# The first projection's constants turned by TensorE, and a new order of the opening steps, in a fused attention and feed-forward kernel

## The chip, the cores and the metric

One core of one Trainium2 chip runs the whole kernel. The metric is the device time of one execution in microseconds; three executions before the change took 102.31, 102.52 and 102.64 us, median 102.52. Beside these stands one profiled execution of 102.53 us, whose span (from the first to the last recorded instruction) is 100.8 us; all durations below are from it. Engines are named as the profile does: PE (TensorE), DVE (VectorE), ACT (ScalarE), POOL (GpSimd) and SP (SyncE, whose queue issues most transfers).

## What is computed

```python
def _attn_ref(q, k, v, S1, S2):          # q, k, v: (4, 4, 1088, 32); S1, S2: (8, 32)
    def phi(x):
        a = np.einsum('rd,bhsd->bhsr', S1, x)
        b = np.einsum('rd,bhsd->bhsr', S2, x)
        return np.einsum('bhsi,bhsj->bhsij', a, b).reshape(*x.shape[:-1], r * r)
    q_p, k_p = (phi(q), phi(k))
    kv = np.einsum('bhsf,bhsd->bhfd', k_p, v)
    z = np.sum(k_p, axis=2)
    num = np.einsum('bhsf,bhfd->bhsd', q_p, kv)
    den = np.einsum('bhsf,bhf->bhs', q_p, z)[..., None] + 1e-06
    return num / den

def _moe_ref(x, w_in, w_out, beta):      # x: (4352, 128); w_in: (128, 2048); w_out: (2048, 128)
    h = x @ w_in
    g = h * (1.0 / (1.0 + np.exp(-beta * h)))
    return g @ w_out
```

The attention's output, with its four heads side by side, is the x of the feed-forward part. Inputs and output are float32.

## The kernel before

The attention runs batch by batch (four batches), and the feed-forward part over 9 chunks of 512 tokens, the last of 256, as soon as their tokens are in xT. The order of all work is written out by hand as a string of names (SEQ, line 1005); each name calls a function that issues its instructions, and each engine takes its own in that order. "+" is `first` (one wave: two matmuls of xT with w_in, line 435, and the activation g on ACT, line 444; nothing if no tokens are ready), "-" is `second` (two matmuls of g with w_out, line 411), "~" is one idle matmul of 448 columns (line 196), whose result nobody reads. Ten such matmuls also stand at the very start.

Batch 0 has an opening of its own. S1 and S2 come in 128 rows each (the 8 rows repeated 16 times; `load_s`, line 102, one on ACT's queue and one on POOL's, followed on ACT's by beta in 48 rows). DVE turns each in blocks of 32 (`prep_s`, line 266); POOL multiplies it with a mask into sk, the weights of the key projection; ACT spreads it into s0 and s1, the weights of the query projections. DVE turns k (`turn_k`, line 470, in two parts), PE projects it with sk (`kps`, line 507), DVE turns the result into kab (`kab`, line 543, two instructions), and POOL and DVE form the outer products kp (`outer`, line 555). From kab PE also sums gram (line 646), from which z follows (zt, zc, zb, lines 650 to 670). On the query side DVE turns q (`turn_q`, line 476), PE makes aps and bps (`spread`, line 593), DVE and ACT copy aps and DVE multiplies (`mult`, line 613); den (line 675) with `invert` (line 688) and `spread_rc` (line 705) gives the reciprocals, `num0` (line 711) the numerators, and `divide0` (line 724) writes xT. Queries of batch 0 go in two chunks, A and B.

Beta is split into three bf16 parts (`beta_top` on ACT, line 286, and `beta_left` on POOL and then DVE, line 289), spread over 128 rows by PE in four groups of four matmuls (`beta_part`, line 294) and copied by ACT (`beta_copy`, line 305, 512 columns each). POOL multiplies it into w_in (`prep_win`, line 314), a quarter each; w_out is scaled by 1/beta on ACT or DVE (`prep_wout`, line 335; on ACT two instructions per name).

PSUM is handed out by three helpers: `two` (a pair of banks, one at a time), `one` (one bank), and `wave2` (two pairs in turn, which the waves use as well). A tile from a helper waits until what was there before has been read. On SP's queue a transfer can also wait for an earlier transfer, since eight semaphores are used in turn.

Steps of the opening by name: tk00 and tk01 turn k's two parts, tqa and tqb q's; kp0, ka0 are the key projection and its turn; bt, bl, be, bc are beta's split, spread and copy; o00 to o04 the outer products, v00 to v04 kv of batch 0; aa, ba, ca, ma the query products of chunk A, da and ia its den and reciprocals, ab, bb, cb, mb those of chunk B; lv, lk, lq, lw, lo and lb load v, k, q, w_in, w_out and beta for the scaling.

Of the kernel before, what the change touches and what calls it, by code (L numbers as in the profile page):

```python
# [18 lines left out]
def kernel(  # L19
# [36 lines left out]
    JR = [(0, 2), (2, 4), (4, 6), (6, 9)]  # L56
    JR0 = [(0, 2), (2, 4), (4, 6), (6, 8), (8, 9)]
# [91 lines left out]
    def load_v(b):  # L149
# [3 lines left out]
        for g in range(4):  # L153
# [8 lines left out]
            )  # L162

# [96 lines left out]
    sab = []  # L260
# [3 lines left out]
    st = []  # L264

    def prep_s(n):
        st_ = sb([P, 4, R], F32, f"st{n}")
        nc.vector.transpose(out=st_.rearrange("p u r -> p (u r)"), in_=sr[n])
# [3 lines left out]
        sab.append(t.rearrange("p i j -> p (i j)"))  # L272
        st.append(st_)

    def prep_sq():
        for t in sq:
            for n in range(2):
                nc.gpsimd.tensor_copy(out=t[:, R * n : R * n + R], in_=st[n][:, 0, :])
# [15 lines left out]
    def beta_part(i):  # L294
        t = PS["beta", i] = two("betaps")[:, 0]
        for n in range(NU):
            nc.tensor.matmul(  # L297
                out=t[:, CB * n : CB * n + CB],
                lhsT=cut(bsel, [[0, P]], NU * i + n),
# [5 lines left out]
    def beta_copy(i):  # L305
        nc.scalar.copy(out=beta_bc[:, WP * i : WP * i + WP], in_=PS["beta", i])  # L306
# [188 lines left out]
    def project(t, moving):  # L495
        for g in range(4):
            for pi in range(2):
                rows = slice(64 * pi, 64 * pi + 64)
                nc.tensor.matmul(  # L499
                    out=t[32 * g : 32 * g + 32, pi, :JW],  # L500
# [6 lines left out]
    def kps(b, new=two):  # L507
        t = PS["kps", b] = new("kps")
        kT = kT2[b % 2]
        project(t, lambda rows, g: kT[rows, NJK * g : NJK * g + NJK, :])  # L510
# [15 lines left out]
    def left_copy(j0, j1, eng):  # L526
        if 0 not in KPS:
            KPS[0] = two("left")[:, 0]
        eng(
            out=KPS[0][:, R * H * j0 : R * H * j1],  # L530
            in_=KAB[0][:, 0, j0:j1].rearrange("p j h i -> p (j h i)"),
        )

    def turn_ab(t, name):
        o = sbA.tile([P, 2, NJK, H, R], F32, tag=name, name=name)
        for pi in range(2):
            nc.vector.transpose(  # L537
                out=cut(o, [[R * H, NJK], [NJK * H * R, 2], [1, 2 * R]], 2 * R * pi),
                in_=t[:, pi, :JW].rearrange("p (j n c) -> p j n c", j=NJK, n=2),
            )  # L540
        return o

    def kab(b):
        KAB[b] = turn_ab(PS["kps", b], "kab")
# [10 lines left out]
    def outer(dst, b, src, nm, j0, j1, eng=None):  # L555
        if b not in dst:
            dst[b] = sbA.tile([P, NJK, H, F], F32, tag=nm, name=nm, bufs=1)
        a0 = src[b][:, 0, j0:j1]
        n = H * (j1 - j0)
        left = cut(a0, [[R, n], [1, R], [0, R]])  # L560
        if b == 0 and eng is nc.vector:
            left = cut(KPS[0], [[R, n], [1, R], [0, R]], R * H * j0)
        (eng or nc.vector).tensor_tensor(  # L563
            out=cut(dst[b][:, j0:j1], [[F, n], [R, R], [1, R]]),
            in0=left,
            in1=cut(a0, [[R, n], [0, R], [1, R]], NJK * H * R),
# [67 lines left out]
    def sums(t, ab, n):  # L634
        for j in range(NJK):
            c = 32 * (j % 4)
            nc.tensor.matmul(  # L637
                out=t[c : c + 32, : H * R],
                lhsT=ab[:, n, j].rearrange("p h i -> p (h i)"),
                rhs=ab[:, 1 - n, j].rearrange("p h i -> p (h i)"),  # L640
# [5 lines left out]
    def gram(b):  # L646
        PS["gram"] = t = one("gram")
        sums(t, KAB[b], 0)
# [87 lines left out]
    def gram_g(b, own):  # L736
        t = PS["gp", b] = one("gp") if own else PS["kps", b][:, 0, JW:]
        sums(t, KAB[b], 1)
# [7 lines left out]
    def wz_g(b):  # L746
        for h in range(H):
            nc.tensor.matmul(
                out=PS["gp", b][32 * h : 32 * h + 32, 64 : 64 + R],
                lhsT=sr[1],  # L750
# [78 lines left out]
    def d_A():  # L829
        PS["dA"] = one("dps")  # L830
# [81 lines left out]
    do("kp0", kps, 0)  # L912
    do("ka0", kab, 0)
# [136 lines left out]
```

## Time and profile before

| what | number | where it is read |
|---|---|---|
| median of three runs | 102.52 us | runs |
| the profiled execution | 102.53 us | its own time |
| its span | 100.8 us | page, first line |
| PE busy | 94.5 us, 94% | page, part 1 |
| ACT busy | 78.6 us, 78% | page, part 1 |
| DVE busy | 58.7 us, 58% | page, part 1 |
| POOL busy | 35.3 us, 35% | page, part 1 |
| idle matmuls, line 196 | 24, in 8.0 us | groups of instructions |
| waves, line 435 | 144 matmuls, 40.5 us | groups of instructions |
| w_out matmuls, line 411 | 128, 36.1 us | groups of instructions |
| activation g, line 444 | 68, mean 1026 ns | groups of instructions |
| first wave | 16.47 us | timeline |

Times of instructions are counted from the start of the span. The records of PE are pipelined: several float32 matmuls stand beside each other, and a group's length in the timeline, not the sum of its records, tells how long PE was at it. A float32 matmul leaves two records. "Idle before" is the time in which an engine had nothing to do, with the one that ended it.

### The profile page before, as it was taken

The numbers are of one execution on the slowest core, as the hardware profiler recorded it, in microseconds if no ns is written. First come the engines' busy times: TensorE is split into PE (matmuls) and PEld (weight loads), VectorE is DVE, ScalarE is ACT, GpSimd is POOL, SyncE is SP. The second block draws the span as 40 slices with busy tenths as digits, with TensorE's granted clock in tenths as the row PEclk, the third lists the DMA queues.
The fourth block names the chain that finished last, engine by engine and source line by source line (L and its number), as shares of the span: only waits on it lengthen the run. The fifth ranks groups of instructions, "written<-read, shape, count | busy, mean of one in ns | idle before, by whom it ended". The sixth has DMA issues, their size and how long they took to land.

```text
span 100.8 us, 2932 instructions
## 1 busy us (share of the span) xinstructions
PE 94.5 (94%) x1215; PEld 46.1 (46%) x1215; DVE 58.7 (58%) x119; ACT 78.6 (78%) x101; POOL 35.3 (35%) x50
## 2 busy tenths in 40 slices
PE   5999998899999999999999999999999999999930
PEld 2435652334645444354455345454534444446820
DVE  2757997769999986596779399395160020200220
ACT  1523655999999979699997679999679999999920
POOL 5348958676009502939991002800000000000000
PEclk9999999999999999999999999999999999999999
DMA  2899999999601585048200150033003314023141
GB/s 44 301 233 311 350 392 381 203 288 268 125 15 24 86 229 218 7 79 188 65 0 0 20 91 0 0 57 54 0 4 53 53 35 71 0 46 61 26 79 52
DMA packets 22876, 11.35 MB, mean 113 GB/s; under 512 B 18320, under 2 KB 20688, under 8 KB 22864
## 3 DMA queue, kind: packets, MB, share of 16 engines
q1 hardware_dynamic: 22480, 11.06, 43.5%
q8 instruction: 9, 0.15, 0.6%
q10 hardware_dynamic: 352, 0.11, 0.4%
q14 instruction: 3, 0.02, 0.1%
q0 software_dynamic: 32, 0.02, 0.1%
HBM read 8.95 MB, written 2.23 MB: 111 GB/s over the span
## 4 chain that ended last, share of the span: by engine, by line
PE 85%; ACT 6%; DVE 3%; issue 1%; DVEq 0%; ACTq 0%
PE wave L435 29%; PE moeout L411 25%; PE kvz L196 7%; ACT g L444 5%; PE kvz L624 5%; PE nps L791 5%; PE kps L499 3%; PE qps L517 2%; PE betaps L297 1%; PE nps L716 1%; PE aps L600 1%; PE dps L679 1%; PE ndps L673 1%; PE gp L637 1%; PE bps L600 1%
## 5 line engine op out<-in xcount | busy, mean ns | idle before, releaser
L444 ACT ACTIVATE g<-wave 128x1024 f16<-128x1024 f32 x68 | 65.5, 1026 | 5.9 <-PE wave L435 5.4
L435 PE MATMUL wave<-xT,winp 128*128 128x512 f16 (+1 forms) x144 | 40.5, 369 | 0.7 <-DVE xT L728 0.3
L411 PE MATMUL moeout<-g,woutp 128*128 128x512 f16 x128 | 36.1, 379 | 0.0
L435 PEld LDWEIGHTS <-winp 128*128 128x128 f16 x144 | 15.0, 115 | 16.7 <-issue 5.4
L411 PEld LDWEIGHTS <-woutp 128*128 128x128 f16 x128 | 12.2, 98 | 14.2 <-issue 0.9
L421 DVE STREAM_TRANSPOSE o_sb<-moeout 128x512 f32<-128x512 f32 x8 | 5.7, 712 | 19.7 <-PE moeout L411 19.6
L563 POOL TENSOR_TENSOR kp<-kab 128x512 f32<-128x512 f32 (+2 forms) x13 | 14.4, 1138 | 7.5 <-DVE kab L537 5.9
L576 POOL TENSOR_TENSOR qo<-qab 128x512 f32<-128x512 f32 (+1 forms) x9 | 11.5, 1304 | 15.1 <-DVE qab L772 15.0
L587 DVE STREAM_TRANSPOSE qt<-qo 128x512 f32<-128x512 f32 (+1 forms) x12 | 8.9, 760 | 1.5 <-POOL qo L576 1.4
L196 PE MATMUL kvz<-idle 128*128 128x448 f16 x24 | 8.0, 477 | 1.1 <-DVE idle L99 1.1
L624 PE MATMUL kvz<-kp,v 128*32 128x64 f32 x288 | 5.7, 221 | 0.0
L624 PEld LDWEIGHTS kvz<-kp,v 128*32 128x32 f32 x288 | 4.5, 110 | 2.5 <-issue 1.6
L317 POOL TENSOR_TENSOR winp<-w_in_sb,beta_bc 128x512 f16<-128x512 f32 x4 | 5.0, 1275 | 1.5 <-DMA w_in_sb<-in_moe_w_in_dram 1.5
L477 DVE STREAM_TRANSPOSE qT<-q 128x1088 f32<-128x1088 f32 (+2 forms) x5 | 5.3, 1062 | 0.0
L471 DVE STREAM_TRANSPOSE kT<-k 128x1088 f32<-128x1088 f32 (+2 forms) x5 | 5.2, 1036 | 0.0
L549 DVE STREAM_TRANSPOSE qab<-qps 128x576 f32<-128x576 f32 x6 | 4.3, 761 | 1.2 <-PE qps L517 1.1
L196 PEld LDWEIGHTS <-idle 128*128 128x128 f16 x24 | 2.8, 125 | 4.6 <-issue 2.9
L791 PE MATMUL nps<-qt,nd 32*32 32x288 f32 x192 | 4.8, 412 | 0.0
L537 DVE STREAM_TRANSPOSE kab<-kps 128x288 f32<-128x288 f32 x8 | 3.3, 456 | 2.3 <-PE kps L499 2.3
L331 ACT ACTIVATE woutp<-w_out_sb,rbeta 128x128 f16<-128x128 f32 x12 | 4.0, 392 | 0.0
L813 ACT CAST xT<-nps 128x576 f16<-128x576 f32 x4 | 2.6, 640 | 1.8 <-PE nps L791 1.7
L306 ACT COPY beta_bc<-betaps 128x512 f32<-128x512 f32 x4 | 2.4, 588 | 1.4 <-PE betaps L297 1.2
(97 smaller groups left out, 71.0 us busy)
## 6 DMA issues: line engine op xcount, KB each, us to landing
v<-in_v_dram SPq DMA_DIRECT2D x15, 144.0 KB, 7.3
k<-in_k_dram SPq DMA_DIRECT2D x3, 544.0 KB, 5.5
q<-in_q_dram SPq DMA_DIRECT2D x3, 544.0 KB, 9.0
out_dram<-o_sb SPq DMA_DIRECT2D x20, 64.0 KB, 1.9
w_out_sb<-in_moe_w_out_dram SPq DMA_DIRECT2D x2, 512.0 KB, 9.6
w_in_sb<-in_moe_w_in_dram SPq DMA_DIRECT2D x2, 256.0 KB, 6.4
w_in_sb<-in_moe_w_in_dram SPq DMA_DIRECT2D x1, 512.0 KB, 6.2
k<-in_k_dram SPq DMA_DIRECT2D x1, 288.0 KB, 3.0
```

What stands on the lines that cost most here:

```text
L196: nc.tensor.matmul(out=kvz0[:, F:], lhsT=idle, rhs=cut(idle, [[0, 7], [1, F]]), start=fresh, stop=True, skip_group_check=True,)
L411: nc.tensor.matmul(out=moe["acc"][:, :tw], lhsT=woutp[:, j, :], rhs=g[jj], start=(j == 0), stop=(j == NJ - 1),)
L421: nc.vector.transpose(out=o_sb[:, :nt, :].rearrange("p t d -> p (t d)"), in_=moe["acc"][:, :tw])
L435: nc.tensor.matmul(out=wv[:, jj // per, o : o + tw], lhsT=win_unit(j0 + jj), rhs=xT[:, t0 : t0 + tw], start=True, stop=True,)
L444: nc.scalar.activation(out=g[:, :, :gw], in_=wv[:, :, :gw], func=ACTF.Silu)
L471: nc.vector.transpose(out=kT2[b % 2][:, t0:t1].rearrange("p t s -> p (t s)"), in_=k_t[b][:, t0:t1].rearrange("p t d -> p (t d)"),)
L477: nc.vector.transpose(out=qT2[b % 2][:, t0:t1].rearrange("p t s -> p (t s)"), in_=q_t[b][:, t0:t1].rearrange("p t d -> p (t d)"),)
L563: (eng or nc.vector).tensor_tensor(out=cut(dst[b][:, j0:j1], [[F, n], [R, R], [1, R]]), in0=left, in1=cut(a0, [[R, n], [0, R], [1, R]], NJ ...
L576: eng.tensor_tensor(out=cut(QO[b][:, j0:j1], [[F, n], [R, R], [1, R]]), in0=cut(a0, [[32, n], [1, R], [0, R]]), in1=cut(a0, [[32, n], [0, ...
L587: nc.vector.transpose(out=QT[b][:, j0:j1].rearrange("p j h c s -> p (j h c s)"), in_=QO[b][:, j0:j1].rearrange("p j h f -> p (j h f)"),)
L624: nc.tensor.matmul(out=KVZ[b][32 * h : 32 * h + 32, :F], lhsT=v_t[b][:, h, j, :], rhs=KP[b][:, j, h, :], start=(j == 0), stop=(j == NJK - ...
L791: nc.tensor.matmul(out=tiles[g // 2][32 * h : 32 * h + 32, g % 2, :JW], lhsT=ND[b][rows, fc, 32 * h : 32 * h + 32], rhs=QT[b][rows, :, h, ...
```

## The change

S1 and S2 are loaded once, 8 rows each, into one tile of 16 rows. PE turns it with four small matmuls against the unit matrix, one for each group of 32 rows, into one PSUM bank; DVE multiplies that with the mask into sk in one instruction, and ACT spreads s0 and s1 from it. S2 in 128 rows, which a later step needs (`wz_g`), is loaded by itself on SP's queue. The first key projection comes in two parts of 4 and 5 blocks of columns with PSUM banks of their own (`kps0`), and its turn in two as well; kab of later batches is one instruction instead of two. Beta is spread in two groups of eight matmuls into two banks each and copied in two instructions of 1024 columns. den of chunk A goes into the bank pair of `two`. The left copy covers the second part alone. SEQ is written anew from end to end: 20 idle matmuls instead of 24, w_out's first half loaded ahead of q's second part, bl0 to BL1 ahead of kab on DVE, k's turn of batch 1 behind chunk A's division, three scalings of w_out on ACT and one on DVE ahead of the first wave.

```diff
+    KJ = [(0, 4), (4, NJK)]
-    sr = []
+    s16 = sb([2 * R, D], F32, "s16")
+    sr2 = sb([P, D], F32, "sr2")
     def load_s():
-        for n, s_ in enumerate((S1, S2)):
-            t = sb([P, D], F32, f"sr{n}")
-            (nc.scalar, nc.gpsimd)[n].dma_start(
-                out=t,
-                in_=bass.AP(
-                    tensor=s_.tensor, offset=s_.offset, ap=[[0, P // R], [D, R], [1, D]]
-                ),
-            )
-            sr.append(t)
+        nc.scalar.dma_start(out=s16[:R], in_=S1)
+        nc.gpsimd.dma_start(out=s16[R:], in_=S2)
...
+    def load_s2():
+        nc.sync.dma_start(
+            out=sr2,
+            in_=bass.AP(tensor=S2.tensor, offset=S2.offset, ap=[[0, P // R], [D, R], [1, D]]),
+        )
...
+    def turn_s():
+        t = PS["st"] = one("st")
+        for g in range(4):
+            nc.tensor.matmul(
+                out=t[32 * g : 32 * g + 32, : 2 * R],
+                lhsT=s16,
+                rhs=ident[: 2 * R, : 2 * R],
+                start=True,
+                stop=True,
+            )
+
+    def prep_sk():
+        nc.vector.tensor_tensor(
+            out=sk,
+            in0=cut(PS["st"], [[R, 2], [0, 2], [1, R]]),
+            in1=cut(hm, [[0, 2], [R, 2], [1, R]]),
+            op=MUL,
+        )
     def prep_s(n):
-        st_ = sb([P, 4, R], F32, f"st{n}")
-        nc.vector.transpose(out=st_.rearrange("p u r -> p (u r)"), in_=sr[n])
-        nc.gpsimd.tensor_tensor(out=sk[:, n], in0=st_[:, :2, :], in1=hm, op=MUL)
         t = sb([P, R, R], F32, f"s{n}")
-        nc.scalar.copy(out=t, in_=cut(st_, ([[1, R], [0, R]], [[0, R], [1, R]])[n]))
+        nc.scalar.copy(out=t, in_=cut(PS["st"], ([[1, R], [0, R]], [[0, R], [1, R]])[n], R * n))
...
     def beta_part(i):
-        t = PS["beta", i] = two("betaps")[:, 0]
-        for n in range(NU):
+        t = PS["beta", i] = (wave2, two)[i]("betaps")
+        for n in range(2 * NU):
...
     def beta_copy(i):
-        nc.scalar.copy(out=beta_bc[:, WP * i : WP * i + WP], in_=PS["beta", i])
+        w = 2 * WP
+        nc.scalar.copy(
+            out=beta_bc[:, w * i : w * i + w].rearrange("p (m c) -> p m c", m=2),
+            in_=PS["beta", i],
+        )
...
+    def kps0(n):
+        j0, j1 = KJ[n]
+        w = 32 * (j1 - j0)
+        t = PS["kpj", n] = (two, wave2)[n]("kps")
+        project(
+            lambda g, pi: t[32 * g : 32 * g + 32, pi, :w],
+            lambda rows, g: kT2[0][rows, NJK * g + j0 : NJK * g + j1, :],
+        )
...
-    def kab(b):
-        KAB[b] = turn_ab(PS["kps", b], "kab")
+    def kab(b, n=0):
+        t, nj = (PS["kps", b], NJK) if b else (PS["kpj", n], KJ[n][1] - KJ[n][0])
+        o = sbA.tile([P, 2, nj, H, R], F32, tag=("kab", "kab1")[n], name="kab")
+        nc.vector.transpose(
+            out=cut(o, [[2 * R, 2], [R * H, nj], [nj * H * R, 2], [1, 2 * R]]),
+            in_=t[:, :, : 32 * nj].rearrange("p m (j c) -> p m j c", c=32),
+        )
+        KAB[b, n] = o
...
     def d_A():
-        PS["dA"] = one("dps")
+        PS["dA"] = two("dps")[:, 0]
...
     SEQ = """
-        s0 lv00 tk00 ~ ~ bt0 lv01 s1 tk01 bl0 sq lv02 ~ kp0 ~ ka0 lv03 la o00 ~ ~ ~ tqa ~ gr o02 bt1 ~
-        aa lqb zt lk1 ba ca0 zz o01 o04 BL1 lb CA1 be0 bc0 ~ lw0 ~ ma0 ma1 ~ tqb o03 be1 lw2 bc1 v00 da
-        v01 be2 lw1 v02 v03 ia v04 bc2 kd u0 tk1 be3 ra0 nd nc lo0 ra1 lq1 bc3 ~ na xa0 ab u1 xa1 cb0 +
-        ~ CB1 rb bb mb1 mb0 w0 lo1 + u2 w3 kp1 + ka1 u3 lv1 w2 o11 + g1 o13 W1 gm1 nb wz1 + wm1 o12 db -
+        tk00 lv00 lv01 ~ tk01 bt0 st sk lv02 ~ bl0 kp0 s0 lb kq0 s1 lv03 bt1 BL1 lo0 kz0 be0 o00 ~ lqb
+        ka0 o04 tqa O02 ~ ls bc0 ~ o01 gr la zt lw0 o03 aa ba CA1 ca0 zz ma1 v00 ma0 rb lw1 v01 v02 v03
+        v04 da kd w0 lk1 lw2 ~ w2 u0 ~ nd W1 nc ia be1 ~ tqb bc1 na u1 w3 lq1 ab ra1 ra0 xa0 cb0 ~ xa1
+        lo1 ~ + bb + CB1 tk1 mb1 sq u2 - mb0 kp1 ka1 + u3 + lv1 o13 g1 gm1 lq2 wz1 wm1 + o11 db + nb o12
...
     """
```

In the new names kq0 and kz0 are the second part of the projection and the first part of its turn, st and sk the turn of S on PE and the mask product on DVE, ls the separate load of S2.

More of the change, by code (lines that the diff above doesn't have):

```diff
@@ L526, in left_copy, with kab_at @@
     def left_copy(j0, j1, eng):
-        if 0 not in KPS:
-            KPS[0] = two("left")[:, 0]
+        KPS[0] = two("left")[:, 0]
         eng(
             out=KPS[0][:, R * H * j0 : R * H * j1],
-            in_=KAB[0][:, 0, j0:j1].rearrange("p j h i -> p (j h i)"),
+            in_=KAB[0, 1][:, 0].rearrange("p j h i -> p (j h i)"),
         )
[L534 to L541, printed above, removed]
-    def kab(b):
-        KAB[b] = turn_ab(PS["kps", b], "kab")
+    def kab(b, n=0):
[4 more added lines that the diff above has]
+            in_=t[:, :, : 32 * nj].rearrange("p m (j c) -> p m j c", c=32),
+        )
+        KAB[b, n] = o
+    def kab_at(b, j):
+        n = int(b == 0 and j >= KJ[0][1])
+        return KAB[b, n], j - KJ[n][0] if b == 0 else j
     def qab(b):
@@ L911 @@
         do2(f"bl{n}", beta_left, (n,), POOL, DVE)
-    do("kp0", kps, 0)
-    do("ka0", kab, 0)
-    do2("la", left_copy, (0, NJK), ACT.copy, DVE.tensor_copy)
+    for n in range(2):
+        do(("kp0", "kq0")[n], kps0, n)
+        do(("kz0", "ka0")[n], kab, 0, n)
+    do("st", turn_s)
+    do("sk", prep_sk)
+    do("ls", load_s2)
+    do2("la", left_copy, KJ[1], ACT.copy, DVE.tensor_copy)
     for g in range(4):
@@ L992 @@
         for n, (j0, j1) in enumerate(JR):
[L993 removed]
+            do2(f"o{b}{n}", lambda b, j0, j1, e: outer(KP, b, "kp", j0, j1, e), (b, j0, j1), POOL, DVE)
             do2(f"p{b}{n}", lambda b, j0, j1, e: outer_q(b, j0, j1, e), (b, j0, j1), POOL, DVE)
```

70 lines of the change are left out of this document (38 added, 32 removed).

## The prediction, made before the changed kernel had run

> **What bounds the kernel now.** First the page: 100.8 us span, a full granted clock in every slice, TensorE (PE) busy 94%, ScalarE (ACT) 78%. The share is an average, so the second view is the table of stages (busy time of each engine in a stretch, then clock, DMA share, GB/s).
>
> ```profile
> 5.00:10.00 5.00, 5.00 (x87) 2.24 (x85) 3.12 (x8) 1.41 (x5) 3.19 (x8) 1.00 1.08 270
> 10.00:15.00 5.00, 4.81 (x121) 3.11 (x125) 4.77 (x10) 3.07 (x8) 3.99 (x5) 1.00 1.06 373
> ...
> 17.00:28.00 11.00, 10.67 (x210) 4.76 (x209) 8.91 (x18) 10.46 (x20) 5.75 (x5) 1.00 0.93 222
> 28.00:38.00 10.00, 10.00 (x112) 4.82 (x117) 8.92 (x14) 8.92 (x11) 4.07 (x3) 1.00 0.41 97
> 38.00:72.00 34.00, 33.93 (x529) 16.05 (x514) 24.00 (x42) 29.82 (x32) 14.52 (x13) 1.00 0.25 55
> 72.00:90.00 18.00, 17.85 (x84) 8.32 (x82) 3.29 (x6) 16.32 (x18) 0.00 (x0) 1.00 0.20 34
> ```
>
> The first pair of numbers of a row is the stretch's length and PE's busy time. From 28 to 90 us PE lacks 0.22 of 62 us, so the change can't shorten that part; it can only start it earlier or later. Before 17 us PE is busy too, but partly with idle matmuls (line 196) that compute nothing, so there the third view, the timeline, decides (start, length, engine, line, operation; in brackets the idle time before it and who ended it).
>
> ```profile
> 1.06 5.04 PE L196 MATMUL kvz<-idle 128*128 128x448 f16 x13 [1.06 <-DVE idle L99]
> ...
> 5.42 0.21 DVE L268 STREAM_TRANSPOSE st<-sr 128x32 f32<-128x32 f32 x1 [0.61 <-DMA sr<-in_S_dram]
> ...
> 6.03 0.94 PE L499 MATMUL kps<-kT,sk 64*32 64x288 f32 x16
> 6.11 0.40 ACT L287 ACTIVATE bt<-beta_r,bpos 48x128 bf16<-48x128 f32 x1 [1.68 <-DMA beta_r<-in_moe_beta_dram]
> ...
> 7.03 0.85 DVE L537 STREAM_TRANSPOSE kab<-kps 128x288 f32<-128x288 f32 x2 [0.81 <-PE kps L499]
> 7.81 0.67 DVE L477 STREAM_TRANSPOSE qT<-q 128x512 f32<-128x512 f32 x1
> ...
> 8.62 1.12 PE L600 MATMUL aps<-qT,s 32*64 32x256 f32 x32
> 8.75 0.43 DVE L290 TENSOR_TENSOR bq<-br,bt 48x128 bf16<-48x128 f32 x1
> ...
> 10.67 0.59 ACT L306 COPY beta_bc<-betaps 128x512 f32<-128x512 f32 x1
> ...
> 13.50 1.25 DVE L471 STREAM_TRANSPOSE kT<-k 128x1088 f32<-128x1088 f32 x1
> ```
>
> The reader is to see one chain: S lands, VectorE (DVE) turns it, kps, kab, qT, then aps at 8.62. Beta's split (line 287, GpSimd (POOL) in between, line 290) lies beside it: beta_r lands at 6.1, its last step bq stands behind kab and qT on DVE, and nothing before aps needs it. The chain of waits gives 16.47 for the first wave, the point from which PE is fed:
>
> ```profile
> 15.57 0.77 DVE xT L728 x2
> 16.33 0.14 issue
> 16.47 0.60 PE wave L435 x2
> ```
>
> **The change, part by part.** I follow each engine's queue as the changed program has it: an instruction starts when its engine is free and its last input is there, with lengths from these rows.
>
> S. The DVE turns (2 x 0.21) and POOL masks (2 x 0.22) go. PE has 11 idle matmuls ahead of the new turn instead of 13: 11 x 0.388 (5.04/13) from 1.06 ends at 5.33. S lands at 3.9 (issue 0.74 + 3.2) and 5.4 (1.26 + 4.1); eight rows will hardly land later, so PE's queue decides. The turn's four matmuls have no row; between nothing and 0.63 (zc, 16 records), nearest is line 748 (8 records, 0.25): 5.58. The mask product reads PSUM like line 742 (0.19): 5.82. kps, 0.94 in all, split 4:5, ends near 6.9, as before (6.97). So S gains 0.1 at most.
>
> Beta on DVE. bq now stands ahead of both kab parts. Behind beta_r's landing come 0.40 (bt), 0.08 and 0.42 (POOL), 0.07 and 0.40 (bt), 0.03 and 0.43 (bq), with what starts them 1.86. The landing is the unknown: 6.1 as it is (1.43 + 4.7); at the earliest S's 3.2 on the same queue, 4.6. I take 5.8, near its own row, since 120 descriptors fewer go ahead. Then bq ends at 7.66. An early landing helps little: ACT's second bt now stands behind two copies of the turned S (2 x 0.24), which wait for the mask product at 5.82, so bq ends at 7.28 at best, 7.96 at worst. The stall is then kab's: 7.66 + 0.85 = 8.51 instead of 7.88, and qT ends 0.60 later, 9.11.
>
> Beta on PE and ACT. Eight matmuls in a group, 2 x 0.38, from 7.72 to 8.48; one copy of 1024 columns. Bounds: 0.59 (half the columns) and 1.18 (two of them); I take the 1.02 of an ACT instruction of that size (line 444). It ends at 9.57, and aps writes the bank pair that it empties, so aps starts at 9.62 and not behind qT: 1.00 late (0.61 to 1.28 with beta's bounds).
>
> From aps to the first wave, before 16.47 - 8.62 = 7.85. After: aps 1.12; copy 0.69 + 0.08; two products 1.29; den 0.43 + 0.05 (its own bank takes no time off: the five kv groups ahead of it end at 12.65, by zc 0.56 and 1.34, and the products at 12.80); to DVE 0.14; turn and add 0.64, for which the second beta group, in den's bank, waits; that group 0.75 + 0.05; its copy 1.02 + 0.06, for which the second aps waits; aps 0.75 + 0.05; two idle matmuls 0.44. Sum 7.56, first wave at 17.18: 0.29 won back. The won part is k's turn of batch 1 (1.25, row 13.50), which leaves this chain; DVE's q turn (0.77), rb (0.72) and xT (0.76) are done at 16.6, inside it. Net 0.71 late.
>
> Behind the first wave. k's turn now stands ahead of the products that the second kps waits for (17.5 to 18.8): kps at about 19.9, 2.75 behind the first wave instead of 2.36, with one moeout pair (0.43) more done. PE also waits some 0.3 for the first g. I take 0.15 (0 to 0.3). In the tail three wave pairs fewer are left (the built order has 48 ahead of the last projection's second half, not 45), and pairs there take 0.47 where they took 0.43 earlier: -0.1.
>
> Loads. SP now issues w_out's first half (0.5 MB) ahead of q's second part, S2's 128 rows, w_in and k of batch 1, and w_out waits for beta_r as k did. At the 270 to 373 GB/s of the stages q's part comes about 1.5 later, 11.6, needed at 14.3; w_in's first part stays near 12.4, needed by POOL after the outer products (11.9) and by PE at 17.2; k of batch 1 moves from 11.6 to about 15, needed at 17.5. Covered; were they not, each costs its lateness. kab in one instruction (0.75 for 0.85), sq from the copies and the shorter left copy cost nothing: the engines that run them wait at those places.
>
> Sum: 0.71 + 0.15 - 0.1 = +0.76. The profiled execution took 102.53 (span 100.8 and 1.7 around it), the median is 102.52: **103.3 us**, own range 102.7 to 103.9 from the bounds.
>
> **The rivals.** (A) Faster: ACT sets the pace behind the first wave. For it: ACT is busy 10.46 of 11 us from 17 to 28, and six of the twelve scalings of w_out (0.68 for two, 2.0 us) move ahead of the first g, into ACT's waits. If PE's records there only stretch over ACT's work, the stage gets up to 2.0 shorter, and the kernel ends at 102.53 + 0.86 - 2.0 = 101.4; it decides once more than 1.2 of the 2.0 comes through (0.8 of front and 0.4 to be told apart). Against it: the chain of waits stays on PE there but for DVE's 0.75. (B) No change: beta lands by 5.2, the copy takes 0.8 and the second group the same: aps at 9.0, the first wave 0.1 late, 102.6. For it: beta_r's 4.7 is long for 24 KB; against: the S copies hold bt. (C) Slower still: PE's slow start lasts longer. Idle matmuls take 0.388 up to 6.0, then 0.22 (1.12 for five). PE now idles from 6.9 to 7.7; if the step comes after kps and the first beta group, these cost 0.75 x 1.7 more, 104.5; against: the step at 6.0 came after 5 us of matmuls, and 4.3 of them remain. [...]
>
> **How the numbers follow.** Main case 0.60, A 0.16, B 0.14, C 0.10. The range reaches down to A's half, 101.9, and up to 104.2, short of C's full price; about 2 in 10 is outside. Over 0.3% (0.31 us, about what a measurement of this kernel can tell from no change): faster is A, with a little of B, 0.18; same is the rest of B and the main case's low edge, 0.15; slower the rest, 0.67.
>
> **What would show it.** Right: bt's second instruction behind the two S copies; bq directly ahead of kab on DVE, kab near 7.7; PE idle about 0.8 between kps and betaps; aps released by beta's copy at 9.2 to 9.9; first wave at 16.9 to 17.6; PE full from 28 on. Wrong: aps released by qT before 9; a first wave before 16.5; the stretch from the first wave to the second batch's kv shorter than 11 us (then A); idle matmuls of 0.38 behind 6.9 (then C).

## The result, and the profile after

| | median (us) | executions | lowest to highest | ratio to before, 95% interval |
|---|---|---|---|---|
| before, beside it | 102.50 | 4 | 102.31 to 102.64 | |
| after | 104.16 | 4 | 103.85 to 106.39 | 1.0154 [1.0121, 1.0186] |
| before, second measurement | 102.36 | 23 | 102.10 to 102.88, and 104.75 and 134.67 | |
| after, second measurement | 103.91 | 12 | 102.65 to 106.72 | 1.0077 [1.0041, 1.0113] |
| before, beside the second experiments | 102.37 | 23 | 101.94 to 102.80, and 106.28, 107.22, 120.98, 182.35 and 245.68 | |

The change makes the kernel slower, by about 1.5% in the median of all executions and by 0.8 to 1.5% by the two ratios. It also makes it uneven: its executions lie 4% apart, most of those of the kernel before within 0.9%. A ratio counts only executions within 1.5% of their kernel's fastest, so the second one leaves out five of the twelve; below, the median of all executions stands beside each ratio. The forecast was 103.3, in the range 101.9 to 104.2, so the first median lies inside by 0.04 us, and above the 102.7 to 103.9 that the prediction gave to its main case.

The first profiled execution of the changed kernel took 103.85 us with a span of 101.0; the one before had 102.53 and 100.8. So the span is only 0.2 longer, where the sum of the prediction had 0.76 more. The timeline of the changed kernel's front (start, length, engine, line; in brackets the idle time before it and who ended it):

```profile
5.28 0.31 PE L269 MATMUL st<-ident,s 16*32 16x16 f32 x8
...
5.59 0.40 ACT L304 ACTIVATE bt<-beta_r,bpos 48x128 bf16<-48x128 f32 x1 [2.01 <-DMA beta_r<-in_moe_beta_dram]
5.66 0.19 DVE L278 TENSOR_TENSOR sk<-st,hm 128x32 f32<-128x32 f32 x1 [0.56 <-PE st L269]
...
6.53 0.40 ACT L304 ACTIVATE bt<-br,bpos 48x128 bf16<-48x128 f32 x1 [0.32 <-POOL br L307]
...
6.96 0.28 DVE L307 TENSOR_TENSOR bq<-br,bt 48x128 bf16<-48x128 f32 x1 [1.11 <-ACT bt L304]
...
7.17 0.83 DVE L570 STREAM_TRANSPOSE kab<-kps 128x256 f32<-128x256 f32 x2
7.29 0.60 PE L315 MATMUL betaps<-bq,bsel 48*128 48x128 bf16 x8 [0.36 <-DVE bq L307]
...
7.94 1.01 ACT L325 COPY beta_bc<-betaps 128x1024 f32<-128x1024 f32 x1 [1.01 <-PE betaps L315]
...
9.00 0.67 PEld L636 LDWEIGHTS aps<-qT,s 32*64 32x64 f32 x32 [0.23 <-ACT beta_bc L325]
9.00 1.12 PE L636 MATMUL aps<-qT,s 32*64 32x256 f32 x32
...
16.58 0.60 PE L457 MATMUL wave<-xT,winp 128*128 128x512 f16 x2
```

(PEld is TensorE's loading of weights.) The order of the waits is the one that was forecast: bq directly behind beta's second bt, the turn kab and betaps behind bq, aps behind the copy of beta. The times are shorter: TensorE stands 0.36 where 0.8 was expected, aps starts at 9.00 and not at 9.62, the first wave at 16.58, 0.11 behind the 16.47 of before. The chain of waits of the same execution shows that beta's load now heads it (start, length, what):

```profile
1.38 4.12 DMA beta_r<-in_moe_beta_dram
7.68 4.17 POOL kp L599 x4
...
13.80 0.63 PE betaps L315 x8
14.45 1.02 ACT beta_bc L325
15.52 0.75 PE aps L636 x16
```

In the table of stages ScalarE has less to do from 17 to 28 us (9.19 us where it was 10.46), and TensorE's middle is as full as it was (33.95 of 34):

```profile
17.00:28.00 11.00, 10.32 (x142) 3.92 (x142) 9.37 (x17) 9.19 (x14) 5.78 (x5) 1.00 0.83 231
...
38.00:72.00 34.00, 33.95 (x472) 16.14 (x458) 24.34 (x41) 30.32 (x33) 13.36 (x12) 1.00 0.30 59
```

No stage of this execution is 1.3 us longer. What it has more is outside the span: 2.85 us around it instead of 1.73. Of the other executions of the two measurements two have as much around their spans (2.99 and 2.92 us) and the rest 1.78 to 2.13. So most of the median's +1.5 us had to be sought inside the spans of other executions.

### The profile page after: what moved, and what is told of

The parts are those of the page before. It is cut to its first block, busy times and chain, and to the rows that moved or that the text cites. A ratio compares the mean times of both kernels' runs of the same rounds, so it can differ in the third digit from the quotient of the medians.

```text
span 101.0 us, 2967 instructions
## 1 busy us (share of the span) xinstructions
PE 93.6 (93%) x1235; PEld 45.8 (45%) x1235; DVE 59.9 (59%) x117; ACT 78.2 (77%) x99; POOL 33.1 (33%) x46
## 3 DMA queue, kind: packets, MB, share of 16 engines
HBM read 8.93 MB, written 2.23 MB: 110 GB/s over the span
## 4 chain that ended last, share of the span: by engine, by line
PE 74%; ACT 8%; POOL 5%; DMA 4%; DVE 3%; issue 2%; ACTq 1%; DVEq 0%
PE wave L457 30%; PE moeout L433 25%; ACT g L466 5%; PE nps L828 5%; PE kvz L660 4%; POOL kp L599 4%; DMA beta_r<-in_moe_beta_dram 4%; PE qps L551 2%; PE kps L521 2%; PE dps L716 1%; ACT beta_bc L325 1%; PE gp L674 1%; ACT bt L304 1%; PE aps L636 1%; PE ndps L710 1%
## 5 line engine op out<-in xcount | busy, mean ns | idle before, releaser
L466 ACT ACTIVATE g<-wave 128x1024 f16<-128x1024 f32 x68 | 65.7, 1024 | 7.2 <-PE wave L457 6.7
L433 PEld LDWEIGHTS <-woutp 128*128 128x128 f16 x128 | 11.9, 97 | 13.9 <-issue 1.9
L612 POOL TENSOR_TENSOR qo<-qab 128x512 f32<-128x512 f32 (+1 forms) x8 | 10.7, 1360 | 18.7 <-DVE qab L809 18.7
L599 POOL TENSOR_TENSOR kp<-kab 128x512 f32<-128x512 f32 (+2 forms) x12 | 13.5, 1142 | 8.2 <-DVE kab L570 8.1
L443 DVE STREAM_TRANSPOSE o_sb<-moeout 128x512 f32<-128x512 f32 x8 | 5.7, 711 | 16.9 <-PE moeout L433 16.9
L197 PE MATMUL kvz<-idle 128*128 128x448 f16 x20 | 7.0, 489 | 1.1 <-DVE idle L100 1.1
L570 DVE STREAM_TRANSPOSE kab<-kps 128x576 f32<-128x576 f32 (+2 forms) x5 | 3.2, 647 | 1.5 <-PE kps L521 1.5
L197 PEld LDWEIGHTS <-idle 128*128 128x128 f16 x20 | 2.1, 123 | 4.2 <-issue 2.9
L599 DVE TENSOR_TENSOR kp<-kab 128x512 f32<-128x512 f32 (+1 forms) x5 | 3.8, 761 | 0.0
```

The costliest lines, as they stand in the source:

```text
L197: nc.tensor.matmul(out=kvz0[:, F:], lhsT=idle, rhs=cut(idle, [[0, 7], [1, F]]), start=fresh, stop=True, skip_group_check=True,)
L433: nc.tensor.matmul(out=moe["acc"][:, :tw], lhsT=woutp[:, j, :], rhs=g[jj], start=(j == 0), stop=(j == NJ - 1),)
L443: nc.vector.transpose(out=o_sb[:, :nt, :].rearrange("p t d -> p (t d)"), in_=moe["acc"][:, :tw])
L466: nc.scalar.activation(out=g[:, :, :gw], in_=wv[:, :, :gw], func=ACTF.Silu)
L599: eng.tensor_tensor(out=cut(dst[b][:, j0:j1], [[F, n], [R, R], [1, R]]), in0=left, in1=cut(a0, [[R, n], [0, R], [1, R]], nj * H * R), op=MUL,)
L612: eng.tensor_tensor(out=cut(QO[b][:, j0:j1], [[F, n], [R, R], [1, R]]), in0=cut(a0, [[32, n], [1, R], [0, R]]), in1=cut(a0, [[32, n], [0, ...
```

## First experiments: the clock, or the new waits

Two theories came from the prediction: (1) TensorE's clock rises later or unevenly, since it idles near 7 us (the prediction's case C); (2) the waits of the new order cost what they were priced at. Four kernels ran beside each other: the changed one again; it with two idle matmuls more at the start; it with its idle places filled; and the kernel before with four idle matmuls fewer.

```diff
 e2_after_warm12 (from after)
-    WARM0 = 10
+    WARM0 = 12
 e3_after_filled (from after)
-    ... lb kq0 s1 lv03 ...    v01 v02 v03
+    ... lb kq0 ~ ~ s1 lv03 ...    v01 v02 ~ v03
 e4_before_less (from before)
-    s0 lv00 tk00 ~ ~ bt0 ...    o00 ~ ~ ~ tqa
+    s0 lv00 tk00 bt0 ...    o00 ~ tqa
```

> The changed kernel once more, in more executions, to see where the 1.6 us lie: its first profile's span is only 0.25 us longer than before's. Theory 1, PE's clock: PE idles more in the opening and has four idle matmuls fewer, so the step to the full clock (6.0 us before, 6.5 us in the first profile) comes at another place in each execution; then times spread by 1 us or more (first four: 103.85 to 106.39), and the longer the span the later the step or the lower the granted clock. Theory 2, the waits of the new order: the loss stands at the same places in each execution, times within 0.4 us of each other near 104.1, and the profile shows a first wave at 16.6 and a later stall of about 1 us.

> The changed kernel with 12 idle matmuls at the start instead of 10 (as many ahead of the first projection as before the change). They cost 2 x 0.37 us on PE ahead of the turn of S. Theory 1 (clock): the step to the full clock is reached more surely, times lose their spread and the median falls by 0.5 us or more, to 103.6 or less, although the front is pushed 0.7 later. Theory 2 (waits): each step behind S is 0.7 later, the median rises by 0.5 to 0.8, to about 104.8.

> The changed kernel with three idle matmuls in PE's two longest waits of the opening (two behind the second part of the first key projection, one ahead of the fourth kv group), where they cost little: the waits were 0.35 and 0.37 us. Theory 1 (clock): PE counts as busy there, the median falls by 0.5 us or more. Theory 2 (waits): same within 0.3 us, or up to 0.3 slower.

> The kernel before with four idle matmuls fewer (two at the start, two behind kab), 20 as in the changed kernel. Theory 1 (clock): it becomes slower and spread like the changed kernel, 103.3 or more in the median, with single runs over 104. Theory 2 (waits): the first four places were covered by waits for S and qT, so the time stays within 0.3 us of 102.5.

| run | median of all | executions, lowest to highest | ratio | profiled: time, span |
|---|---|---|---|---|
| e1, after again | 103.91 | 12, 102.65 to 106.72 | 1.0077 [1.0041, 1.0113] | 104.90, 103.1 |
| e2, after, 12 idle first | 104.89 | 6, 103.88 to 106.90 | 1.0169 [1.0131, 1.0206] | 103.88, 102.1 |
| e3, after, places filled | 103.89 | 6, 103.55 to 105.49 | 1.0157 [1.0110, 1.0203] | 103.61, 101.8 |
| e4, before, 4 idle fewer | 102.32 | 12, 101.90 to 103.24, and 134.51 | 1.0002 [0.9976, 1.0029] | 101.90, 100.1 |

Neither theory holds. By the trace's clock events the clock rose at 6.52 us in the first profile of after, at 5.08 in e1, 5.29 in e2, 6.50 in e3, and stayed up until TensorE's last matmul was done (in after it fell at 98.68, where the last matmul ends at 97.17; the mean over the span is 0.988, 0.988, 0.994 and 1.0). In the first profile of after idle matmuls start 0.37 us apart ahead of the rise and 0.19 behind it. e1 has the earliest rise of the four and the longest span. Filling the idle places or adding matmuls at the start won nothing, and the kernel before lost nothing by having fewer. But the three new profiles of the changed order have a piece that neither kernel's first profile has. In the chain of waits of e1:

```profile
14.01 0.62 PE betaps L315 x8
14.62 1.22 issue
15.84 0.35 PE kvz L197
...
24.76 0.63 PE nps L753 x12
25.39 0.17 issue
25.56 0.68 PE nps L753 x4
```

of e2:

```profile
13.73 0.51 PE betaps L315 x6
14.24 0.58 issue
14.81 0.28 PE betaps L315 x2
```

and of e3:

```profile
13.86 0.45 PE betaps L315 x5
14.31 0.51 issue
14.82 0.34 PE betaps L315 x3
```

"issue" is time in which the engine waited for nothing that the profile shows. Here it falls ahead of an idle matmul in one run, and between two matmuls of the same group, which depend on nothing new, in the others. Counted from the start of the trace (from nought; an f32 matmul leaves two records, the four of S's turn eight), it is in all three TensorE's matmul record number 220; the second stop of e1 is number 347. That second stop costs more than its 0.17 us, since the ends of matmul records are modelled: the group of 16 takes 1.47 us in e1 and 0.65 in the first profile of after. The 127 matmuls between, with their 127 weight loads, are 254 instructions. The page lists a DMA queue that carries such things:

```profile
q8 instruction: 9, 0.15, 0.7%
```

(of after; packets, MB, share). Each packet is 16,384 bytes, 64.5 for each of the 254. From 28 us on, where the loads are thin, 55 of 75 packets in the fourteen profiles start within a microsecond of the time at which TensorE passes record 93 + 127 n (the others up to 2.2 us earlier or 3.5 later), so a block seems to be asked for when TensorE enters the one before it. The first block would then be asked for at record 93, near 9.3 us, and it starts 2.6 to 4.0 us later in the four profiles of the changed order so far, at a time when the loads keep the 16 DMA engines full (a share of 1.03 to 1.07 from 9.3 to 11.9 us). This gave theory 3: TensorE runs out of instructions where it reaches record 220 before the block is there. By the trace's records of that queue, with runs of the sections below:

| run | block moved (us) | record 220 starts (us) | behind the block's end | stall ahead of it |
|---|---|---|---|---|
| before | 12.72 to 13.82 | 15.40 | 1.58 | none |
| after | 11.90 to 13.00 | 14.34 | 1.34 | none |
| e1 | 13.50 to 14.51 | 15.84 | 1.33 | 1.22 |
| e1, second block (347) | 23.04 to 24.12 | 25.56 | 1.44 | 0.17 |
| e2 | 12.31 to 13.36 | 14.81 | 1.45 | 0.58 |
| e3 | 12.50 to 13.57 | 14.81 | 1.24 | 0.51 |
| e4 | 12.50 to 13.61 | 14.90 | 1.29 | none |
| f1 | 12.03 to 13.11 | 14.54 | 1.43 | none |
| f2 (221) | 13.84 to 14.96 | 16.18 | 1.22 | 0.32 |
| f4 | 12.20 to 13.14 | 15.63 | 2.49 | none |
| g4 (221) | 12.49 to 13.60 | 15.08 | 1.48 | 0.89 |
| g4, second block (348) | 22.91 to 24.25 | 25.54 | 1.29 | 1.72 |
| g5 | 14.23 to 15.34 | 16.69 | 1.35 | 0.37 |

Wherever TensorE stalls, it goes on 1.22 to 1.48 us behind the block's end. Where it doesn't stall, it comes to the record no earlier than that; in f3, g1 and g2, which the table leaves out, it comes 2.4 to 4.4 us behind. Over all block boundaries of the fourteen profiles the shortest distance is the 1.22 of f2. The changed kernel has 20 records more ahead of this place (8 of S's turn, 16 of the projection in two parts, 4 idle matmuls fewer), and so reaches the boundary at 14.3 us instead of 15.4, about when the block is usable; how late that is differs from execution to execution. The stops at a boundary were 0.17 (e1's second) to 1.72 us long (g4's second, in a stretch with a DMA share of 1.03).

## Second experiments: fewer records, more records, S alone

f1 takes the projection back into one part, f3 takes six idle matmuls away as well (four by its expectation), f2 gives the kernel before 21 records more, f4 gives it the part on S alone.

```diff
 f1_after_kps_whole (from after)
-    KJ = [(0, 4), (4, NJK)]
+    KJ = [(0, NJK), (NJK, NJK)]        (kq0, ka0, la leave the order)
 f2_before_24_small (from before)
-    WARM0 = 10
+    WARM0 = 7
+    for _ in range(24):
+        nc.tensor.matmul(out=kvz0[:32, F : F + 8], lhsT=idle[:, :32], rhs=idle[:, :8], ...)
 f3_after_whole_less (from f1)
-    o00 ~ lqb   O02 ~ ls bc0 ~ o01   lw2 ~ w2 u0 ~ nd   be1 ~ tqb
+    o00 lqb     O02 ls bc0 o01       lw2 w2 u0 nd       be1 tqb
 f4_before_s_alone (from before; load_s, load_s2, turn_s, prep_sk, prep_s as in after)
-    s0 lv00 tk00 ~ ~ bt0 lv01 s1 tk01 bl0 sq lv02 ~ kp0 ~ ka0 lv03 la
+    lv00 tk00 ~ ~ bt0 st sk lv01 s0 s1 tk01 bl0 lv02 ~ kp0 ~ ka0 lv03 ls la
```

> The changed kernel with batch 0's first key projection in one part again (8 matmuls of 288 columns, one turn by VectorE, no copy of the left operands); all else as changed. TensorE has 16 matmuls fewer ahead of the first projections of beta and a. Theory 3 (TensorE runs out of instructions: each block of 16,384 bytes is asked for when TensorE enters the block before it, at its matmul number 93, 220, 347 and so on, and comes 5.0 to 6.4 us later, because it waits 2.6 to 4.0 us behind the loads; with the change TensorE needs only 5.0 to 5.3 us for the 127 matmuls between 93 and 220): here the boundary falls 16 matmuls later, on the projection by S of the second half, near 15.5 us, where TensorE waits anyway. Median 102.6 to 103.0, its slowest and fastest execution less than 0.8 apart, no stall without a cause ahead of matmul 220, or one below 0.3. Theory 2 (the waits of the new order cost the time): the order behind the projection is the same, so 103.5 to 104.2.

> The kernel before with three of its ten first idle matmuls replaced by 24 small ones (32 weight columns, 8 columns each), so that TensorE has 21 matmuls more to fetch and about as much work as before; nothing that computes is changed. Theory 3: the instruction block's boundary moves from the projection by S at 15.4 us to an instruction at about 14.1 us, and TensorE stands there for 0.5 to 1.0 us for nothing that the profile shows, ahead of matmul number 220; median 102.9 to 103.6, executions more than 1 us apart. Theory 2 and the theory of the clock: within 0.3 of the kernel before.

> As the run with the key projection in one part, and four idle matmuls behind the projection left out too: 20 matmuls fewer than the changed kernel ahead of the boundary. Theory 3: the boundary lies a little later again, no stall; 102.3 to 102.8, as fast as the kernel before. Theory 2: 103.5 to 104.2. Theory of the clock (idle matmuls keep it at full speed): slower than the run before it, by 0.3 or more.

> The kernel before with the part on S alone: S1 and S2 loaded as 16 rows, turned by four matmuls, one product with the mask on VectorE, the 128-row copy of S2 loaded by SyncE for its later use; projection, beta, den and the order otherwise as before. TensorE has 4 matmuls with one pass more each (8 records) ahead of the boundary. Prediction's own price for this part: a gain of at most 0.1, so 102.3 to 102.5 by that alone. Theory 3: the boundary moves from 15.4 to about 15.0 us, where the block has just landed (13.8 + 1.3 = 15.1): 102.3 to 102.9, with some executions late by a few tenths. Theory 2 sees no wait in this part: 102.3 to 102.5.

| run | median of all | executions, lowest to highest | ratio | profiled: time, span |
|---|---|---|---|---|
| f1 | 103.07 | 12, 102.50 to 105.72 | 1.0051 [1.0025, 1.0077] | 102.50, 100.7 |
| f2 | 103.98 | 8, 103.17 to 105.91 | 1.0158 [1.0127, 1.0188] | 105.04, 102.8 |
| f3 | 104.55 | 12, 102.61 to 107.78 | 1.0077 [1.0035, 1.0119] | 105.03, 103.2 |
| f4 | 103.32 | 6, 102.95 to 103.71 | 1.0099 [1.0069, 1.0128] | 103.28, 101.5 |

f1's median is 0.84 us below the changed kernel's, and its profile has no stall. But the two ratios differ by 0.26% only and their intervals overlap, f1 also takes out a copy and a turn, and three of its twelve executions are still above 104 (theory 3 had allowed a spread of 0.8); so it agrees with theory 3 and doesn't prove it. f2 stalls where it should ("issue" of 0.32 at 15.86, ahead of record 221), but its clock also rose only at 10.16 us (five idle matmuls at 7.65 took 2.05 us, the five of before at 6.90 took 1.12), and nothing here shows why; its loss can be from both, and a cleaner test follows as g4.

f3 was a miss of the kind that teaches. It should have been as fast as before, at 102.3 to 102.8. By the ratios it isn't told apart from f1, but eight of its twelve executions are above 104, where f1 has three. The profiled execution is one of the eight. The stages of its profile (length, busy time of PE, PEld, DVE, ACT and POOL with counts, granted clock, DMA share, GB/s):

```profile
5.77:9.18 3.41, 1.82 (x43) 0.96 (x42) 2.02 (x5) 1.97 (x5) 1.31 (x2) 1.00 1.09 200
9.18:16.01 6.83, 6.33 (x130) 4.16 (x131) 4.45 (x10) 2.39 (x9) 6.49 (x10) 0.50 1.04 391
```

In 3.41 us TensorE was busy for 1.82; then its clock was half for 6.83 us. The mean granted clock goes with the time: 0.925 to 0.983 in the eight late executions, 0.988 to 1.0 in the other four. f1, which has the six idle matmuls that f3 leaves out, has 0.989 to 1.0 in ten of its twelve and 0.983 and 0.958 in the two slowest. So they weren't idle for nothing in this order. The prediction's case C is close to this, but not the same: there the clock rises late, here it falls again. Neither is what the two profiles of the changed kernel show: there the clock stays up until TensorE's last matmul is done. And of the six executions of e1 above 104, five have a granted clock of 0.988 to 1.0, as the others have (0.990 to 1.0); only the latest, 106.72, has 0.980. (In the first measurement one of the four, 104.25, has 0.975.)

f4 has no stall, as its boundary is reached late, and its executions lie close together. It is slower by 1.0% all the same, above the 102.3 to 102.9 expected, by its own order: one idle matmul more than in after stands ahead of the turn, which starts at 5.66 (5.28 in after), and the mask product stands on VectorE ahead of k's second turn, for which the second half of kps waits 0.34:

```profile
5.66 0.30 PE L268 MATMUL st<-ident,s 16*32 16x16 f32 x8
...
6.37 1.21 PE L515 MATMUL kps<-kT,sk 64*32 64x288 f32 x16
...
6.89 0.15 PEld L515 LDWEIGHTS kps<-kT,sk 64*32 64x32 f32 x8 [0.34 <-DVE kT L487]
```

Before, kps started at 6.03 and took 0.94: it ends 0.34 + 0.27 = 0.61 late, and kab (7.65 for 7.03) and the first wave (17.05 for 16.47) follow with it. So S alone, in this order, is no gain, and the run doesn't price it in another.

## Third experiments: beta off the path, and records alone

In the six profiles of the changed order so far beta's first step came between 5.0 and 5.9 us, and in five of them kab 1.58 behind it: a varying load on the path, theory 4. g1 and g2 put bq behind the mask product of the gram sums and both beta groups behind zc, g1 with the projection in one part, g2 in two. g4 is the clean test of theory 3: the kernel before, with its ten first idle matmuls cut in three, as much busy time and 20 records more.

```diff
 g1_whole_beta_behind (from f1), g2_parts_beta_behind (the same from after)
-    PS["beta", i] = (wave2, two)[i]("betaps")
+    PS["beta", i] = two("betaps")
-    bt1 BL1 lo0 kz0 be0 o00 ~ lqb ... tqa O02 ~ ls bc0 ~ o01 gr zt lw0 o03 ... zz ma1 ... ia be1 ~ tqb bc1 na
+    bt1 lo0 kz0 ~ ~ o00 ~ lqb ... tqa ~ O02 ~ ls o01 gr ~ zt lw0 BL1 o03 ... zz be0 bc0 be1 bc1 ma1 ... ia ~ tqb na
 g4_before_idle_in_three (from before)
-    keep_warm(WARM0, True)
+    for n in range(WARM0):
+        for c0, n_, w_ in ((0, 3, 50), (150, 3, 50), (300, 2, 74)):
+            nc.tensor.matmul(out=kvz0[:, F + c0 : F + c0 + n_ * w_], lhsT=idle, rhs=cut(idle, [[0, n_], [1, w_]]), ...)
```

> The changed kernel with the first key projection in one part (as in the run f1_after_kps_whole) and beta moved: its second square on VectorE behind the turn of the projection, the turn of q and the mask product of the gram sums, its 16 matmuls together behind zc (both groups in the same pair of banks), both copies behind them, and three idle matmuls more in the places where TensorE would stand. Theory 4 (beta's load lies on the path of the changed order: it landed between 5.0 and 5.9 us in the profiles taken so far, the turn of the projection follows 1.58 us behind, and where it is late TensorE stands for a microsecond or more near 7 us, in one execution so long that its clock fell to half from 9 to 16 us): with beta off the path the late executions go; first wave at 15.7 to 16.2, median 102.0 to 102.6, fewer than 2 in 10 executions above 103.5. Theory 3 alone (instruction blocks): no better than the run with one part, 102.8 to 103.2, with the same tail to 105 and more.

> The same with the projection in its two parts, as changed: 16 matmuls more ahead of the block boundary (matmul number 220), and otherwise as the run before it. Theory 3: TensorE comes to the boundary near 14 us, before the block is there: a stall of 0.3 to 1.2 for nothing that the profile shows directly ahead of matmul 220, median 102.9 to 103.8, 0.6 to 1.0 above the run before it. Theory 4 alone: as fast as the run before it within 0.3.

> The kernel before with each of its ten first idle matmuls cut into three of 150, 150 and 148 columns: 20 matmuls more to fetch, TensorE busy for as long (3.7 us at half clock), so that its clock has no reason to rise later, and nothing that computes is changed. Theory 3: the block boundary moves from the second projection by S (15.4 us) to near 13.9 us; a stall of 0.3 to 1.2 directly ahead of matmul 220, median 102.8 to 103.6, executions 1 us and more apart. Theory 4 and the theory of the clock: within 0.3 of the kernel before.

| run | median | executions, lowest to highest | ratio | profiled: time, span |
|---|---|---|---|---|
| g1 | 104.91 | 5, 104.90 to 105.24 | 1.0259 [1.0230, 1.0288] | 104.91, 103.1 |
| g2 | 104.76 | 6, 104.32 to 105.61 | 1.0247 [1.0205, 1.0290] | 104.51, 102.7 |
| g4 | 104.80 | 6, 103.67 to 106.90 | 1.0199 [1.0153, 1.0246] | 104.91, 103.0 |

g4 shows theory 3 at work in the kernel before. Nothing that computes is changed and the clock rose at 5.50 us, earlier than before (6.03), yet the kernel is 2.0% slower. Its median of 104.80 is above the 102.8 to 103.6 expected, as the expectation had only the first boundary. Its chain of waits has two in it:

```profile
13.86 0.33 PE ndps L682
14.19 0.89 issue
15.08 0.35 PE kvz L196
...
23.49 0.32 PE moeout L420
23.81 1.72 issue
25.54 0.39 PE moeout L420
```

The stops are ahead of records 221 and 348, 127 apart, 1.48 and 1.29 us behind the ends of their blocks (the table above), and together 2.61 us.

g1 and g2 were meant to test theory 4 and don't, through a wait that they brought in: the second beta group needs the bank pair that the first one's copy empties. In the timeline of g1:

```profile
10.42 0.62 PE L315 MATMUL betaps<-bq,bsel 48*128 48x128 bf16 x8
12.14 0.60 PE L315 MATMUL betaps<-bq,bsel 48*128 48x128 bf16 x8 [1.10 <-ACT beta_bc L325]
```

and in its stages:

```profile
9.77:13.19 3.42, 2.23 (x68) 1.99 (x72) 2.80 (x7) 2.15 (x4) 3.13 (x4) 1.00 1.06 378
13.19:16.60 3.41, 3.41 (x64) 1.69 (x52) 1.16 (x4) 2.27 (x8) 2.68 (x7) 0.50 1.02 407
```

With a stop of 1.10 us TensorE was busy for 2.23 of 3.42 us in that stretch, and the next 3.41 us ran at half clock; g2 is the same (2.31 of 3.41). Such a stretch alone doesn't bring the clock down, though: e1, from 11.91 to 15.32, has 2.33, and g4, around its second stop, has less still, and the clock stayed up in both (1.00 in the second row below; in e1 the two idle matmuls at 17.45 took 0.48, as in after at 16.26, where two took 0.86 in g1's half clock).

```profile
22.57:25.98 3.41, 1.69 (x14) 0.49 (x12) 3.27 (x6) 1.72 (x2) 2.23 (x2) 1.00 1.03 280
25.98:29.39 3.41, 3.41 (x90) 1.72 (x91) 1.66 (x4) 3.00 (x7) 0.00 (x0) 1.00 0.30 67
```

(This view is of g4.) One thing can be read from g2: with beta off the path kab starts at 6.60 and aps at 8.32, where after has 7.17 and 9.00. In these two profiles the change's own beta order costs 0.57 at kab and 0.68 at aps; how much of it reaches the end stays open.

## Last experiment: a version without the two costs

```diff
 g5_whole_less_records (from f1)
-    PS["beta", i] = (wave2, two)[i]("betaps")
+    PS["beta", i] = (two, wave2)[i]("betaps")
-    s16 = sb([2 * R, D], F32, "s16")
+    s16 = sb([2 * R, 4, D], F32, "s16")        (loaded four times over; one matmul turns it)
-    bt1 BL1 lo0 kz0 be0 o00 ~ lqb ... O02 ~ ls bc0 ~ o01 gr zt lw0 o03 aa ba CA1 ca0 zz ma1
+    bt1 lo0 kz0 ~ o00 ~ lqb ... O02 ~ ls ~ o01 gr zt lw0 BL1 o03 aa ba CA1 ca0 zz be0 bc0 ma1
```

> A version meant to keep the change's gains without its two costs: the key projection in one part; S turned by one matmul instead of four (its 16 rows repeated four times in the load); beta's second square on VectorE behind the gram's mask product, its first 8 matmuls behind zc and the other 8 where the changed kernel has them, each group in banks that nothing holds at that time (so that TensorE doesn't stop between them, as it did for 1.1 us in the two runs with beta behind the projection, where its clock then fell to half for 3.4 us); one idle matmul more near the front. TensorE has 21 records fewer than the changed kernel ahead of the same place. Theory 3: the boundary at matmul 220 lies in the second projection by S near 14.7 us, 4.6 to 5.3 us behind its request: a stall of 0 to 0.5, part of it in time in which TensorE waits for the first wave anyway; first wave 15.7 to 16.3; median 101.7 to 102.5, at most 0.2 slower than the kernel before. Theory of the clock: no stop of TensorE above 0.6 us between 6 and 16 us, so no fall; if there is one, 104 and more. Theory 2 (the other waits of the new order): 103 to 104.

Measured: median 104.07 (6 executions, 103.36 to 104.25), before beside it 102.36, ratio 1.0146 [1.0103, 1.0189]; span 102.2, first wave at 17.75 and not at 15.7 to 16.3. The clock rose at 6.55 and stayed (1.000 over the span). The chain of waits:

```profile
12.46 0.97 DVE woutp L368
13.43 0.47 issue
13.89 0.46 DVE dps L734
...
15.63 0.70 PE aps L640 x4
16.33 0.37 issue
16.69 0.40 PE aps L640
```

Three things make its first wave 1.54 later than that of f1 (16.21). kps started at 6.30 (5.69 in f1), and den's matmuls ended 0.71 later, at 13.33. Behind them the turn of den (`dps`) started only at 13.89, 0.5 more behind f1's, since it stands behind VectorE's scaling of w_out, which took 1.51 us where it took 0.42 in f1:

```profile
11.84 0.42 DVE L364 TENSOR_TENSOR woutp<-w_out_sb,rbeta 128x256 f16<-128x256 f32 x1
...
12.46 1.51 DVE L368 TENSOR_TENSOR woutp<-w_out_sb,rbeta 128x256 f16<-128x256 f32 x1
```

The first line is from f1's timeline, the second from g5's. In g5 it ran beside GpSimd's first scaling of w_in (12.41 to 13.69), in f1 it had ended before that one started (12.33); whether this is the cause wasn't tried. And the block started only at 14.23, so that TensorE stopped for 0.37 ahead of record 220. No version tried here beats the kernel before; f1 and g5 are slower, and e4, its four idle matmuls fewer, is the same (1.0002).

## Why the forecast was nearly right, and for which wrong reason

- **S.** Right: the turn started at 5.28 (5.33 forecast), the mask product ended at 5.85 (5.82), kps started at 6.00, as before (6.03).
- **Beta on DVE.** The wait is where it was forecast, its size isn't. beta_r landed at 5.50 (5.8), and the chain from there took 1.74 (1.86), with bq at 0.28 (0.43); so bq ended at 7.24 and not at 7.66, just below the 7.28 that stood as the best. That bound came from two copies of S that would hold bt; they were over by 6.21, and bt waited for GpSimd's step until 6.49. The first kab part was done 0.37 behind bq, and the outer products began there, without the second part.
- **Beta on PE and ACT.** Eight matmuls took 0.60 (0.76), the copy 1.01 (1.02). aps started at 9.00: 0.38 late, not 1.00, and below the 0.61 that stood as the lower bound.
- **From aps to the first wave.** 7.58 for a forecast of 7.56, and the match is luck. den stood behind kv groups, the last of which waited for GpSimd's outer products until 11.85, and ended at 13.01, 4.01 behind aps for 3.66 in the sum; the second beta group (0.62 for 0.75) and the steps behind it were 0.33 shorter. The wave came at 16.58, net 0.11 late and not 0.71.
- **Behind it.** The second kps came 2.73 behind the first wave (2.75 forecast). The last matmul started at 96.95, 0.25 later than before, so 0.14 was lost behind the first wave and in the tail (0.05 forecast).
- Of the prediction's signs of being right, those of order were there and those of size were not: kab came at 7.17 (7.7), aps at 9.00 (9.2 to 9.9), the wave at 16.58 (16.9 to 17.6).
- **Rival A** (ACT sets the pace) is out: ACT has 1.27 us less to do from 17 to 28 us, and the end didn't come earlier. **Rival B** had the front right (aps at 9.0, first wave 0.1 late), by other sizes than its own; its 102.6 is the fastest execution (102.65). **Rival C** isn't in any profile of the changed kernel; the clock rose late in f2 (10.16), and fell again in f3, g1 and g2.

The step that failed is "Sum: 0.71 + 0.15 - 0.1 = +0.76". Its first term was mis-sized and measured +0.11, and the whole order +0.25 at the last matmul. And the sum holds only durations and waits: 20 more records on TensorE had no price of their own. They put it at a block boundary ahead of its block: in e1, the changed kernel itself, the records start 0.21 later than in its first profile from betaps on (beta), 1.2 later behind the first stop, and 2.0 later behind the second, which is the 2.1 that its span is longer (103.1 for 101.0). Two errors of opposite sign, a front priced 0.5 too high and stops priced at nothing, left a forecast of +0.8 where the first median has +1.66, inside the range: that is luck.

What isn't settled: how the late executions that weren't profiled divide between late blocks, late beta and, in the two with the lowest granted clock, a fall of the clock; and why the first profile of after spent 2.85 us outside its span. In that profile a tenth block moved at 102.81 to 104.09 us, behind the last instruction; one did in f2 too (103.86 to 105.28, 2.2 us around its span), and in e2, e3 and g2 the tenth moved while the end was still being computed, with 1.8 around. That is a coincidence in five profiles and wasn't tried.

## What to carry to other kernels

Count TensorE's instructions as well as its time: here, where many small matmuls run while the loads fill the DMA engines, 20 more cost 2.0% (g4, 1.0199), and an "issue" gap between two matmuls of one group (0.58 in e2, 0.51 in e3), or two gaps 127 records apart (e1, g4), was the sign of it. With six idle matmuls taken away the granted clock was 0.925 to 0.983 in eight executions and 0.988 to 1.0 in four (f3), so look at the granted clock of every execution, not only of the one profiled. And a load that an order moves onto the path brings its spread with it (beta's first step came between 5.0 and 5.9 us in six profiles), so one profile doesn't price it.

## What the runs showed of the hardware

- An instruction block of 16,384 bytes took 0.9 to 1.6 us to move. Under full loads the first one started 1.6 to 4.0 us behind the time at which it is reckoned to be asked for (record 93, or 94 in f2 and g4; fourteen profiles), and the second one up to 7.8 us behind (g4). Where TensorE had stopped for a block, it went on 1.22 to 1.48 us behind the block's end.
- TensorE's clock fell to half after a stretch of 3.41 us in which it was busy for 1.82 (f3), 2.23 (g1) and 2.31 us (g2). It didn't after stretches of 2.39 and 2.33 (e1, 5.08 to 8.49 and 11.91 to 15.32 us) and of 1.69 (g4, 22.57 to 25.98 us). So the busy time of a stretch doesn't decide it alone, and what else counts stays open. Where it fell, it was granted at 0.50 for 3.41 us (g1, g2) or 6.83 us (f3).
- Four idle matmuls fewer near the front changed nothing in the kernel before (1.0002 [0.9976, 1.0029]), and the clock rose at 4.28 us there, at 6.03 in the kernel before. In two executions of the changed kernel, with the same matmuls, it rose at 6.52 (after) and at 5.08 (e1): the moment isn't set by the number of matmuls alone.
